# Row norms from 32-row blocks on four column tiles, a re-balanced order and a fourth buffer, in a residual quantizer kernel

## The chip, the cores and the metric

The kernel runs on one core of a Trainium2 chip. The metric is the device time of one execution in microseconds (us). The runs of the kernel before all lie between 754.28 and 757.95 us. All times compared here are of runs taken beside runs of the kernel before on the same chip. Engines: PE is TensorE (matmuls; PEld its weight loads), DVE is VectorE, ACT is ScalarE, POOL is GpSimd, SP issues the input transfers. PSUM is the memory that TensorE writes and VectorE and ScalarE read; the kernel uses it in banks of 512 columns, and emptying it is called an eviction. The trace gives the clock granted to TensorE as full or half (its records hold 1.0 or 0.5); "half clock" is the time spent at half.

## The reference

```python
# x: 2 x 16000 x 512 bf16; codebooks: 4 stages x 8 codes x 512
z = silu(depthwise_conv3(x, dw_enc))
res, q = z, 0
for s in range(4):
    d2 = norm2(res)[..., None] - 2 * res @ cb[s].T + norm2(cb[s])
    sel = cb[s][d2.argmin(-1)]
    q, res = q + sel, res - sel
return depthwise_conv3(q, dw_dec)
```

The norm of a row does not alter which code is nearest, but it takes part in the bf16 rounding of the distances, so the kernel computes it.

## The kernel before

The 32,000 rows go through in tiles of up to 16 groups of 128 rows. For each tile VectorE and ScalarE compute z (transposed: the 512 columns lie on partitions, four chunks of 128). Scores for stages 0 to 2 and the norms come from one "score block" on TensorE; stage 3, which needs the rounded residual, gets a second one. Between them lie 24 residual updates per tile: TensorE multiplies one-hot rows by codebooks into PSUM, and either VectorE adds the result to z (one matmul per PSUM bank) or ScalarE copies it back, for which TensorE must first add z itself with an identity matmul.

A score block for 8 row groups uses z as weights and as moving data, in blocks of 64 rows on two column tiles. The diagonal of each 64 x 64 product is the norm; a mask of -2^100 off the diagonal, laid down by one matmul per bank first, lets a maximum pick it out.

```python
# z buffer: [128, KT, 2*GM, 96]; each 64-row block carries its 32 codebook columns (times -2)
for u in range(nb):                  # row groups of this PSUM bank
    for i in range(KT):              # 4 chunks of 128
        for h in range(2):           # two column tiles of 64
            blk = Z[:, i, 2 * (g0 + nb * q + u) + h, :]
            nc.tensor.matmul(o[64 * h:64 * h + 64, u * w:(u + 1) * w],
                             lhsT=blk[:, NC:ZW], rhs=blk[:, c0:ZW], ...)   # 96 or 72 moving columns
# VectorE then empties it:
nc.vector.tensor_reduce(out=rr[0], in_=v[:, :, :, NC:ZW], axis=X, op=max)      # 64 wide
nc.vector.tensor_tensor(out=S, in0=v[:, :, :, 0:24], in1=CC2, op=add)
```

A list scheduler in the kernel file (class `Plan`) orders all steps with estimated costs. It has tuned ranks (`WHEN`), limits on evictions outstanding per engine (`QUOTA`), and a bias (`SHARE`) that decides whether a residual update is evicted by VectorE or ScalarE. Its estimates decide the order alone: in the program each engine's instructions then stand in that fixed order.

## Time and profile before

| | before |
|---|---|
| time, median of 3 | 756.12 us |
| VectorE busy / idle of the span | 719.4 / 35.0 us |
| ScalarE busy | 640.0 us |
| TensorE busy | 549.0 us |
| a score block, mask to last matmul, mean of 63 calls | 2.15 us |
| TensorE at half clock | 89 us |

The groups of instructions by shape of the kernel before; columns are line, engine, operation, output and inputs, shapes and count, then busy us and mean ns of one, then idle time of the engine before them and what ended it:

```profile
L626 ACT CAST ZB<-ps 128x1024 bf16<-128x1024 f32 x213 | 202.9, 1032 | 18.7 <-PE ps L620 17.2 <-ACT ZB L626 0.7 <-DVE rr L521 0.7
...
L628 DVE TENSOR_TENSOR ZB<-ZB,ps 128x1024 bf16<-128x1024 bf16 x123 | 146.8, 1210 | 5.0 <-PE ps L620 5.0
...
L521 DVE TENSOR_REDUCE rr<-ps 128x8 f32<-128x512 f32 x30 | 20.5, 682 | 1.7 <-PE ps L486 1.7
...
L645 DVE TENSOR_REDUCE rr<-ps 128x8 bf16<-128x512 f32 x30 | 20.4, 681 | 1.8 <-PE ps L486 1.8
```

An eviction costs VectorE 1210 ns and ScalarE 1032 (L628, L626). The two norm reductions take 682 ns each, and VectorE waited less than 2 us in all before each group of thirty: TensorE had the blocks ready. How far ahead it was shows in the timeline (start us, duration us, then as above; a bracket gives idle time and its cause). First VectorE, then TensorE (the second bank of a block and what follows it), of the same stretch of the kernel before:

```profile
390.67 0.74 DVE L446 TENSOR_SCALAR TA<-XT,WENC 128x2048 bf16<-128x2048 bf16 x1
391.33 1.41 DVE L446 TENSOR_SCALAR TB<-XT,WENC 128x2048 bf16<-128x2048 bf16 x2
392.65 0.68 DVE L521 TENSOR_REDUCE rr<-ps 128x8 f32<-128x512 f32 x1
```

### The profile page before, as it was taken

What the parts mean: (1) busy time and instruction counts of PE and PEld (TensorE: products, weight loads), DVE (VectorE), ACT (ScalarE), POOL (GpSimd) and SP (SyncE); (2) the same over time, 40 slices, a digit from 0 to 9 for tenths busy, and PEclk for the clock granted to TensorE, in tenths of its full rate; (3) what the DMA queues carried; (4) which work ended last, traced back from release to release, by engine and by line L of the source; (5) the groups of instructions that cost most, each with busy time, mean ns of one, the idle gap of its engine ahead of it and who ended that gap; (6) DMA issues with size and microseconds to landing.
All of it is one profiled execution on the core that took longest, in us unless ns stands there. A gap on an engine that the chain in (4) does not pass through costs nothing. (4 is left out here: it accounts for less than half of the span.)

```text
span 754.4 us, 15788 instructions
## 1 busy us (share of the span) xinstructions
PE 549.0 (73%) x6425; PEld 281.0 (37%) x6425; DVE 719.4 (95%) x1286; ACT 640.0 (85%) x549; POOL 131.8 (17%) x199
## 2 busy tenths in 40 slices
PE   1163667777786777888777778887777878898994
PEld 0131234243342434444343434444343434453442
DVE  8989999999999999999999999999999999989992
ACT  7776897939799698998989899898989899988575
POOL 2002212000120213112021212202131211111113
PEclk9996697999999999899999999999999999999998
DMA  5443434402333334242433424242432220212214
GB/s 114 98 99 76 117 60 111 99 9 57 84 113 84 114 77 148 50 106 86 97 120 73 146 57 121 70 112 93 91 128 56 101 54 30 85 56 86 85 56 149
DMA packets 148016, 67.27 MB, mean 89 GB/s; under 512 B 139776, under 2 KB 139808, under 8 KB 147944
## 3 DMA queue, kind: packets, MB, share of 16 engines
q1 hardware_dynamic: 137088, 33.06, 20.5%
q0 software_dynamic: 10640, 32.78, 12.7%
q8 instruction: 50, 0.82, 0.5%
q10 hardware_dynamic: 216, 0.43, 0.2%
q14 instruction: 22, 0.18, 0.1%
HBM read 0.43 MB, written 32.77 MB: 44 GB/s over the span
## 5 line engine op out<-in xcount | busy, mean ns | idle before, releaser
L620 PE MATMUL ps<-OHW,CBN 128*128 128x512 bf16 (+1 forms) x768 | 268.6, 391 | 42.4 <-DVE ZB L628 34.4
L626 ACT CAST ZB<-ps 128x1024 bf16<-128x1024 f32 (+2 forms) x281 | 236.2, 918 | 35.0 <-PE ps L620 32.6
L619 PE MATMUL ps<-ZB,IDENT 128*128 128x512 bf16 (+1 forms) x494 | 194.1, 393 | 36.3 <-DVE ZB L628 16.8
L628 DVE TENSOR_TENSOR ZB<-ZB,ps 128x1024 bf16<-128x1024 bf16 (+2 forms) x151 | 162.7, 1098 | 5.1 <-PE ps L620 5.0
L620 PEld LDWEIGHTS <-CBN 128*128 128x128 bf16 x768 | 76.2, 100 | 186.4 <-issue 122.5
L709 POOL DMA_DIRECT2D out_dram<-YB x130 | 70.1, 543 | 376.9 <-ACT YB L686 374.0
L686 ACT CAST YB<-ps 128x1024 bf16<-128x1024 f32 x126 | 121.4, 1031 | 17.0 <-PE ps L678 14.6
L455 ACT ACTIVATE EX<-ZB 128x4096 bf16<-128x4096 bf16 (+2 forms) x36 | 115.5, 3209 | 12.8 <-DVE ZB L298 11.7
L486 PE MATMUL ps<-ZB 128*64 128x96 bf16 (+1 forms) x4032 | 106.7, 210 | 21.3 <-DVE ZB L298 21.1
L486 PEld LDWEIGHTS <-ZB 128*64 128x64 bf16 x4032 | 90.0, 116 | 71.1 <-issue 42.1
L467 ACT ACTIVATE EX<-EX 128x4096 bf16<-128x4096 bf16 (+2 forms) x36 | 115.0, 3198 | 0.2
L678 PE MATMUL ps<-WDEC,OHW 128*128 128x512 bf16 x252 | 75.7, 391 | 28.4 <-DVE PR L543 6.9
L446 DVE TENSOR_SCALAR TB<-XT,WENC 128x2048 bf16<-128x2048 bf16 (+2 forms) x144 | 95.1, 678 | 0.0
L619 PEld LDWEIGHTS <-IDENT 128*128 128x128 bf16 x494 | 49.9, 101 | 64.7 <-issue 14.1
L298 DVE TENSOR_TENSOR ZB<-ZB,EX 128x4096 bf16<-128x4096 bf16 (+2 forms) x36 | 72.6, 2016 | 1.1 <-ACT EX L467 1.0
L298 DVE TENSOR_TENSOR TA<-TA,TB 128x4096 bf16<-128x4096 bf16 (+2 forms) x36 | 72.9, 2024 | 0.1
L298 DVE TENSOR_TENSOR ZB<-TA,TB 128x4096 bf16<-128x4096 bf16 (+2 forms) x36 | 72.5, 2014 | 0.0
L429 POOL COPY XT<-XT 128x508 bf16<-128x508 bf16 x18 | 36.3, 2018 | 124.3 <-DVE TB L446 120.8
L481 PE MATMUL ps<-MSK,IDENT 128*128 128x288 bf16 (+2 forms) x126 | 40.6, 323 | 20.4 <-DVE S L522 15.4
L455 ACT ACT_TABLE_LOAD x17 | 21.8, 1283 | 37.1 <-DVE ZB L298 37.0
L446 DVE TENSOR_SCALAR TA<-XT,WENC 128x2048 bf16<-128x2048 bf16 (+2 forms) x72 | 51.8, 728 | 0.4 <-issue 0.2
L678 PEld LDWEIGHTS <-OHW 128*128 128x128 bf16 x252 | 24.1, 99 | 60.8 <-issue 40.2
(92 smaller groups left out, 447.7 us busy)
## 6 DMA issues: line engine op xcount, KB each, us to landing
out_dram<-YB POOLq DMA_DIRECT2D x33, 448.0 KB, 3.4
out_dram<-YB POOLq DMA_DIRECT2D x28, 512.0 KB, 3.0
XT<-in_x_dram SPq DMA_TRANSPOSE x252, 2.8
out_dram<-YB POOLq DMA_DIRECT2D x30, 60.0 KB, 3.4
out_dram<-YB POOLq DMA_DIRECT2D x31, 2.0 KB, 2.8
out_dram<-YB POOLq DMA_DIRECT2D x2, 224.0 KB, 2.7
YB<-in_dw_dec_dram ACTq DMA_DIRECT2D x1, 384.0 KB, 3.9
out_dram<-YB POOLq DMA_DIRECT2D x1, 384.0 KB, 3.9
```

The source lines that it names most:

```text
L298: add("DVE", cost, key, lambda: nc.vector.tensor_tensor(out=out, in0=a, in1=b, op=op), reads, writes, **kw)
L446: return lambda: nc.vector.tensor_scalar(out=dst, in0=X[:, i, k:k + G, :].rearrange("p g c -> p (g c)"), scalar1=WENC[:, k, i:i + 1], scal ...
L455: add("ACT", act(2 * R), ("exp", n, h), lambda: nc.scalar.activation(v(ex), Z, ACT.Exp, scale=-1.0), zt, [("EX", sl), "ACTTAB"], hold="E")
L467: nc.scalar.add_instruction(mybir.InstActivation(name=nc.get_next_instruction_name(), engine=mybir.EngineType.Activation, func=ACT.Reciprocal,
L486: nc.tensor.matmul(o[HB * h:HB * h + HB, u * w:(u + 1) * w], lhsT=blk[:, NC:ZW], rhs=blk[:, c0:ZW], start=False, stop=(u == nb - 1 and i = ...
L619: nc.tensor.matmul(o.rearrange("p (k h c) -> p k h c", h=2, c=HB), lhsT=IDENT, rhs=zg[:, k0:k0 + nk], start=True, stop=False)
L620: nc.tensor.matmul(o, lhsT=CBN[s, u][:, i * P:(i + 1) * P], rhs=W[:, k0:k0 + nk, PADC:PADC + P], start=not on_act, stop=True)
L626: nc.scalar.copy(zg, v)
L628: nc.vector.tensor_tensor(out=zg, in0=zg, in1=v, op=ALU.add)
L678: nc.tensor.matmul(o, lhsT=W[:, k, PADC:PADC + P], rhs=WDEC[u], start=True, stop=not wrap)
L686: add("ACT", act(1024), key, lambda k=k, box=box, Y=Y, k0=k0: nc.scalar.copy(Y[:, 2 * (k - k0):2 * (k - k0) + 2, :].rearrange("p g d -> p ...
L709: nc.gpsimd.dma_start(out=view[p0:p1, lo:hi, :], in_=Y[p0:p1, lo - g0:hi - g0, :])
```

## The change

The intent was to cut VectorE's work in two ways. Row norms come from 32-row blocks, so that VectorE reduces over 32 columns instead of 64; TensorE uses four column tiles, with twice as many instructions of 64 moving columns each. And the order was re-tuned, moving 20 full evictions from VectorE to ScalarE. The codebook columns no longer stand in every z block but once per buffer, and a moving access pattern of two pieces joins them to the block. This makes z smaller and contiguous, one PSUM bank holds 8 row groups, and a fourth z buffer fits.

```diff
-    HB = P // 2
+    HB = 32
-    NX, NE, NZ, NOH, NY = 2, 3, 3, 4, 4
+    NX, NE, NZ, NOH, NY = 2, 3, 4, 4, 4
-    QUOTA = {"ACT": 2, "DVE": 2}
+    QUOTA = {"ACT": 2, "DVE": 1}
     (SHARE, SLACK and all ranks WHEN: other numbers; cut)
-    ZB = [sb([P, KT, 2 * GM, ZW], BF16, f"ZB{b}") for b in range(NZ)]
+    ZF = [sb([P, ZN + KT * NC], BF16, f"ZB{b}") for b in range(NZ)]
...
-                    for h in range(2):
-                        blk = Z[:, i, 2 * (g0 + nb * q + u) + h, :]
-                        nc.tensor.matmul(o[HB * h:HB * h + HB, u * w:(u + 1) * w], lhsT=blk[:, NC:ZW], rhs=blk[:, c0:ZW], ...)
+                    for q in range(P // HB):
+                        blk = Z[:, i, b0 + u, HB * q:HB * (q + 1)]
+                        at = (i * GM + b0 + u) * P + HB * q
+                        both = bass.AP(tensor=blk.tensor, offset=blk.offset, ap=[blk.ap[0], (ZN + i * NC - at, 2), (1, HB)])
+                        nc.tensor.matmul(o[HB * q:HB * (q + 1), u * ZW:(u + 1) * ZW]..., lhsT=blk, rhs=both, ...)
...
-                nc.vector.tensor_reduce(out=grp(rr[0], ...), in_=v[:, :, :, NC:ZW], axis=AX.X, op=ALU.max)
+                nc.vector.tensor_reduce(out=rr[0][:, g0:g1, 0], in_=v[:, :, 0:HB], axis=AX.X, op=ALU.max)
```

## The prediction

> **What bounds it now.** VectorE. The page's busy table has DVE at 719.4 us of the 754.4 us span (95%), ACT 640.0, PE 549.0. In windows of 42 us from 84 to 671 us DVE is 40.5 to 41.95 busy; tiles of 16 row groups follow each other every 43.3 us (spacing of the score matmuls in the timeline). DVE's 35 us of idle time lie mostly in the first two and the last windows (4, 3 and 17 us).
>
> **What changes, by durations from the trace.**
> 1. Row norms. The 60 full norm reductions read 8x64 PSUM columns in 682 ns; the 192-column score addition takes 346, the 64-column cast 213. Between these a column costs about 1.05 ns, so 8x32 should take about 415 ns: with the small tiles 16.4 us less DVE.
> 2. Residual evictions. The instruction order shows 20 full ones (and one small) moved from DVE (about 1.18 us busy each) to ACT (about 1.0): DVE -24 us, ACT +21. A middle tile has 7 instead of 8 on DVE.
> 3. Setup. Twelve ACT copies of codebook columns (1.08 us each) become 16 tiny ones: ACT -9 us, at the start.
> 4. PE. A score block goes from two column tiles of 96 or 72 moving columns to four of 64. A pair now repeats every 43 ns (96) or 33 ns (72), its halves 3 ns apart[...]. Four tiles should repeat every 30 to 38 ns: for 8 row groups 1.0 to 1.2 us plus a 0.22 us mask matmul, against 2.1 (96) and 1.75 (72) now: twice the instructions, yet about 35 us less PE over 60 calls; 40 more identity matmuls cost 9. PE isn't the limit. One PSUM bank instead of two per call and a fourth z buffer loosen waits.
> 5. Contiguous z changes no DVE rate: additions into strided z take 2280 ns, into contiguous TA 2282.
>
> **Sum.** DVE 719 - 16 - 24 = 679; ACT 640 + 21 - 9 = 652. A middle tile: DVE about 42.6 - 1.07 - 1.18 = 40.4, ACT about 38.8 + 1.0 = 39.8. Nearly level, so each has less slack to wait: I put the tile at 41.0 us, 2.3 less over 12 tiles = 28 us. Of the other 12 us of removed DVE work, at head and tail, I count 7. 756 - 35 = 721 us. Nearly all of the DVE saving is on the critical path; the PE saving hardly.
>
> **Prediction: 721 us, 8 in 10 between 708 and 737; faster by over 2%: 0.92, within 2%: 0.07, slower: 0.01.**
>
> **What would show it.** Right: norm reductions at 400 to 430 ns; DVE busy 675 to 685, still the fullest engine at about 94%; ACT 645 to 658; score quads 28 to 38 ns apart; middle tiles 40.5 to 41.5 us apart; DVE idle 38 to 48 us. Wrong: reductions over 500 ns; quads at 50 ns or more, with PE waits before the reductions; DVE idle over 60 us.
>
> **What would make it wrong.** Four column tiles might not load weights in parallel, and PE grow by over 60 us, delaying the decisions. DVE with only one eviction outstanding might wait for PE more often. With DVE and ACT level, each may stall on the other, leaving 735 to 745. Or the fourth buffer removes more idle time at head and tail than I count, to 705.

The 30 to 38 ns are the author's estimate. The trace of the kernel before alone leads to about the same: 24 columns more (96 against 72) cost a pair 10 ns, so 64 columns on two tiles would take about 30 ns, and two further tiles, each 3 ns behind as the second half of a pair is, about 36.

## More of the kernel before

```profile
389.66 0.34 PE L481 MATMUL ps<-MSK,IDENT 128*128 128x384 bf16 x1
389.92 0.87 PE L486 MATMUL ps<-ZB 128*64 128x96 bf16 x32
390.80 0.38 PE L619 MATMUL ps<-ZB,IDENT 128*128 128x512 bf16 x1
```

The block ends at 390.79 and VectorE starts to reduce it at 392.65. Over all 64 blocks the median of this lead is 1.85 us.

A few lines of the page of the kernel before: the span, each engine's busy time with its share of the span and its instructions, and the queue that fetches instructions (packets, MB, share of the transfer engines).

```profile
span 754.4 us, 15788 instructions
...
PE 549.0 (73%) x6425; PEld 281.0 (37%) x6425; DVE 719.4 (95%) x1286; ACT 640.0 (85%) x549; POOL 131.8 (17%) x199
...
q8 instruction: 50, 0.82, 0.5%
```

VectorE is busy 95% of the time: it is the limit. The last line looks harmless, but it matters later: queue q8 moved 50 packets of 16,384 bytes, and TensorE ran 12,850 instructions (6,425 matmuls and as many weight loads), about 257 to a packet.

## The result and the profile after

The changed kernel took 765.51 us (762.97 to 767.38, 4 runs) beside 755.75 us for the kernel before: a ratio of 1.0127, 95% interval 1.0093 to 1.0161. It is slower by 1.3%. (Ratios are the mean time of one kernel's runs over the mean of the other's in the same rounds, so not quite the ratio of the medians.)

The same lines of the page, and of the groups by shape, of the changed kernel:

```profile
span 765.6 us, 23805 instructions
...
PE 539.3 (70%) x10436; PEld 269.8 (35%) x10436; DVE 684.1 (89%) x1265; ACT 648.0 (85%) x574; POOL 132.3 (17%) x199
...
q8 instruction: 81, 1.33, 0.7%
```

```profile
L492 PE MATMUL ps<-ZB 128*32 128x64 bf16 x8064 | 92.9, 205 | 44.2 <-DVE ZB L306 22.9 <-issue 21.1
...
L644 DVE TENSOR_REDUCE rr<-ps 128x8 bf16<-128x256 f32 x30 | 12.5, 418 | 18.7 <-PE ps L591 9.7 <-PE ps L492 7.3 <-PE ps L559 1.3
L521 DVE TENSOR_REDUCE rr<-ps 128x8 f32<-128x256 f32 x30 | 12.5, 416 | 12.3 <-PE ps L492 10.8 <-PE ps L591 1.4
```

The work fell almost as predicted: a norm reduction takes 416 to 418 ns, VectorE is busy 684.1 us, ScalarE 648.0. But VectorE's idle time rose from 35.0 to 81.5 us, more than the 35.3 us of work that it lost. 31 us of its waits are now before the norm reductions (3.5 before), for TensorE. And TensorE's score matmuls have 21.1 us of idle time under "issue", which means time in which the engine waited for nothing that the profile shows; before they had none.

Such a stretch in the timeline of the changed kernel, TensorE first, then VectorE:

```profile
349.93 0.38 PE L492 MATMUL ps<-ZB 128*32 128x64 bf16 x25
351.14 1.58 PE L492 MATMUL ps<-ZB 128*32 128x64 bf16 x103 [0.83 <-issue]
352.65 1.89 PE L677 MATMUL ps<-WDEC,OHW 128*128 128x512 bf16 x4
354.33 0.50 PE L485 MATMUL ps<-MSK,IDENT 128*128 128x512 bf16 x1
354.75 0.33 PE L492 MATMUL ps<-ZB 128*32 128x64 bf16 x20
355.96 1.20 PE L492 MATMUL ps<-ZB 128*32 128x64 bf16 x108 [0.88 <-issue]
356.98 0.64 PE L591 MATMUL ps<-IDENT,OHA 128*32 128x128 bf16 x20
359.69 0.27 PE L591 MATMUL ps<-IDENT,OHA 128*32 128x128 bf16 x4 [2.08 <-issue]
```

```profile
352.75 0.42 DVE L521 TENSOR_REDUCE rr<-ps 128x8 f32<-128x256 f32 x1 [1.85 <-PE ps L492]
...
360.00 0.42 DVE L644 TENSOR_REDUCE rr<-ps 128x8 bf16<-128x256 f32 x1 [4.36 <-PE ps L591]
```

TensorE stops in the middle of a score block, between two matmuls that depend on nothing new, and again 256 instructions later (a matmul and its weight load are two). VectorE stands still behind it. The last reduction waits even for the transposes L591 behind its block: in the trace the block's last matmul sends no semaphore update of its own, the next update is that of the last transpose, and a stop had fallen between them.

Counting TensorE's matmuls and weight loads in the trace shows where the stops fall. 21 gaps of more than 0.6 us without a wait (from the start of one instruction to that of the next) add up to 28.9 us. The longest is 2.33 us. All 21 end at the same place in the count, 191 past a multiple of 256, so they lie whole multiples of 256 instructions apart; queue q8 moved 81 packets (called refills below) for TensorE's 20,872 instructions, about 258 to a packet. The packet of q8 before each stop's end starts 2.26 to 2.9 us before TensorE goes on. Two packets never start less than 3.35 us apart, while an undisturbed score block of 8 row groups runs its 256 score instructions in 1.22 us. In the kernel before there is no such gap at all. That TensorE waits there for its next packet is inferred from these counts and times; no record names the cause.

**Theory.** The doubled score instructions outrun the instruction fetch, and the stops land on VectorE because the re-balanced order has taken away the lead that used to hide such things. **Rivals.** (a) The re-tuned order or the levelled engines alone: each stalls on the other. (b) 32-wide column tiles are slow. (c) The fourth buffer starts transfers earlier, which then collide with others (the share of busy transfer engines in the middle windows rose from about 0.37 to about 0.5). (d) TensorE's half-clock time, up from 89 to 116 us.

### The profile page after: what moved, and what is told of

The parts are those of the page before. It is cut to its first block, busy times and chain, and to the rows that moved or that the text cites. A ratio compares the mean times of both kernels' runs of the same rounds, so it can differ in the third digit from the quotient of the medians.

```text
span 765.6 us, 23805 instructions
## 1 busy us (share of the span) xinstructions
PE 539.3 (70%) x10436; PEld 269.8 (35%) x10436; DVE 684.1 (89%) x1265; ACT 648.0 (85%) x574; POOL 132.3 (17%) x199
## 4 chain that ended last, share of the span: by engine, by line
DVE 59%; PE 26%; issue 8%; ACT 4%; DMA 1%; SPq 1%; DVEq 0%; POOL 0%; POOLq 0%; ACTq 0%
DVE ZB L627 12%; DVE ZB L306 11%; DVE TB L455 8%; PE ps L492 8%; PE ps L619 7%; DVE TA L306 6%; PE ps L618 5%; DVE TA L455 4%; DVE EX L465 3%; PE ps L677 2%; DVE OHW L595 2%; PE ps L485 2%; DVE KEY L306 2%; DMA XT<-in_x_dram 1%; ACT YB L685 1%
## 5 line engine op out<-in xcount | busy, mean ns | idle before, releaser
L625 ACT CAST ZB<-ps 128x1024 bf16<-128x1024 f32 (+2 forms) x302 | 257.6, 938 | 56.2 <-PE ps L619 54.8
L618 PE MATMUL ps<-ZB,IDENT 128*128 128x512 bf16 (+1 forms) x535 | 210.0, 393 | 28.7 <-DVE ZB L627 10.3
L708 POOL DMA_DIRECT2D out_dram<-YB x130 | 79.4, 615 | 435.3 <-ACT YB L685 432.5
L627 DVE TENSOR_TENSOR ZB<-ZB,ps 128x1024 bf16<-128x1024 bf16 (+2 forms) x130 | 139.0, 1087 | 6.4 <-PE ps L619 5.9
L685 ACT CAST YB<-ps 128x1024 bf16<-128x1024 f32 x126 | 126.3, 1038 | 13.3 <-PE ps L677 12.5
L492 PE MATMUL ps<-ZB 128*32 128x64 bf16 x8064 | 92.9, 205 | 44.2 <-DVE ZB L306 22.9
L492 PEld LDWEIGHTS <-ZB 128*32 128x32 bf16 x8064 | 81.3, 100 | 106.2 <-issue 82.3
L485 PE MATMUL ps<-MSK,IDENT 128*128 128x512 bf16 (+1 forms) x64 | 26.8, 419 | 29.9 <-DVE S L522 14.5
L437 POOL COPY XT<-XT 128x508 bf16<-128x508 bf16 x18 | 19.4, 1081 | 143.8 <-DMA XT<-in_x_dram 122.6
L465 DVE TENSOR_SCALAR EX<-EX 128x4096 bf16<-128x4096 bf16 (+2 forms) x36 | 39.0, 1083 | 1.0 <-ACT EX L464 1.0
L438 POOL COPY XT<-XT 128x508 bf16<-128x508 bf16 x18 | 30.7, 1706 | 47.4 <-DVE TB L455 38.5
```

The lines of the kernel that those rows point to most:

```text
L492: nc.tensor.matmul(o[HB * q:HB * (q + 1), u * ZW:(u + 1) * ZW].rearrange("p (s c) -> p s c", s=2), lhsT=blk, rhs=both, start=False, stop=( ...
L618: nc.tensor.matmul(o, lhsT=IDENT, rhs=zg[:, k0:k0 + nk, :], start=True, stop=False)
L625: nc.scalar.copy(zg, v)
L627: nc.vector.tensor_tensor(out=zg, in0=zg, in1=v, op=ALU.add)
L685: add("ACT", act(1024), key, lambda k=k, box=box, Y=Y, k0=k0: nc.scalar.copy(Y[:, 2 * (k - k0):2 * (k - k0) + 2, :].rearrange("p g d -> p ...
L708: nc.gpsimd.dma_start(out=view[p0:p1, lo:hi, :], in_=Y[p0:p1, lo - g0:hi - g0, :])
```

## The experiments

### 1. Half the score instructions (e1_half)

Two column tiles of 64 weights, each with the two pieces of 32 moving columns. Half the norms are wrong. VectorE and ScalarE run the same instructions in the same order as in the changed kernel.

```diff
-                    for q in range(P // HB):
-                        blk = Z[:, i, b0 + u, HB * q:HB * (q + 1)]
-                        at = (i * GM + b0 + u) * P + HB * q
+                    for q in range(2):
+                        blk = Z[:, i, b0 + u, 64 * q:64 * (q + 1)]
+                        at = (i * GM + b0 + u) * P + 64 * q
```

> The changed kernel with its score blocks on two column tiles of 64 weights (moving pieces still 2 x 32 columns): half the score instructions of TensorE (4,032 weight loads and 4,032 matmuls instead of 8,064 each), same array time per block, same order and sizes on every other engine. The norms of half the rows are wrong on purpose; the sizes read from PSUM are not. Instruction fetch theory (TensorE runs out of instructions at 16 KB boundaries): refills fall from 81 to about 50, the no-wait gaps vanish, VectorE idle falls from 81 us to about 40, 718 to 732 us. Rival (the new order, or VectorE and ScalarE being level, makes each stall on the other): 758 to 770 us.

Measured: 738.19 us (ratio to before 0.9762, interval 0.9739 to 0.9785). From the page of this run, the busy times and the instruction queue:

```profile
PE 531.0 (72%) x6404; PEld 265.6 (36%) x6404; DVE 684.1 (93%) x1265; ACT 646.7 (88%) x574; POOL 132.0 (18%) x199
...
q8 instruction: 50, 0.82, 0.5%
```

The gaps fell from 21 to one, and VectorE's idle time from 81.5 to 52.3 us at the same busy time, 684.1. So the count of instructions costs 27 us of the changed kernel (765.5 to 738.2), and rival (a) alone is refuted. The clock is no part of this: half-clock time is 111 us here and 116 in the changed kernel. But it is not all: the figure lies between the two expectations, 17 us above the prediction.

### 2. Twice the score instructions in the kernel before (e2_before_quads)

```diff
-                    for h in range(2):
+                    for h in range(4):
                         blk = Z[:, i, 2 * (g0 + nb * q + u) + h // 2, :]
-                        ...matmul(o[64 * h:64 * h + 64, ...], lhsT=blk[:, NC:ZW], rhs=blk[:, c0:ZW], ...)
+                        r0 = NC + 32 * (h % 2)
+                        ...matmul(o[32 * h:32 * h + 32, ...], lhsT=blk[:, r0:r0 + 32], rhs=blk[:, c0:ZW], ...)
```

> The kernel before with each 64-row score matmul split into two of 32 rows on four column tiles, all with the same moving columns (96 or 72): twice the score instructions, about the same array time (a quad about 6 ns longer than a pair), the same result, schedule and work on every other engine. Instruction fetch theory: about 81 refills, stalls of 0.5 to 2.3 us at some of them, VectorE idle up by 15 to 45 us, 770 to 800 us. Rival (schedule or balance): 754 to 760 us, as before.

Measured: 760.55 us (ratio 1.0055, 1.0031 to 1.0078), correct. This misses the fetch theory's expectation and lies just above the rival's. The waits of this run (who waited for whom: us in total, times, longest):

```profile
PE ps L487 <- issue: 25.2, 24, 2.4
...
DVE rr L646 <- PE ps L487: 6.0, 5, 2.3
...
DVE rr L522 <- PE ps L487: 3.9, 3, 2.8
```

The stops are all there: 81 refills, 27 gaps, 34.0 us in sum, more than in the changed kernel. Yet they cost about 4 us. So the stops alone don't explain the loss; the kernel before absorbs them, and the changed kernel does not. That made the second half of the theory, the lead, the question to test. The run also speaks against rival (b): its quads of 96 columns repeat every 42 to 43 ns, just as the pairs of the kernel before do.

### 3 and 4. The old ranks, and three z buffers (e3_old_schedule, e4_three_z)

The changed kernel with `SHARE`, `SLACK`, `QUOTA` and `WHEN` of the kernel before; and the changed kernel with `NZ` = 3.

> The changed kernel with the ranks, shares, slacks and quotas of the kernel before. Schedule theory: the new numbers are the fault, the time falls to 720 to 735 us. Instruction fetch theory: the score bursts stay as dense, so the time stays at 750 to 785 us, with 81 refills and no-wait gaps of 20 to 40 us in sum.

> The changed kernel with three z buffers instead of four. If the fourth buffer is the fault (earlier loads, DMA share 0.5 instead of 0.37 in the middle windows): 745 to 758 us. Instruction fetch theory: the fourth buffer is not the fault, 762 to 785 us.

Measured: 803.46 us (1.0627) and 835.49 us (1.1041), both correct, both with 81 refills. Both are far worse than the changed kernel and outside all their expected ranges. They tell little: the scheduler makes a different order from each set of numbers, and these sets were not tuned for it, so the two runs clear neither the new numbers nor the fourth buffer. Half-clock time was 161 and 218 us. Against rival (c) speak other runs: experiment 1 keeps the fourth buffer and transfer engines as busy (0.39 to 0.55 in the windows from 213 to 553 us, 0.42 to 0.52 in the changed kernel) and gains 27 us, and experiment 12 will show the stops with three buffers. For the other 17 us rival (c) is not excluded.

### 5. Empty instructions put back (e5_pad)

Experiment 1 with a second matmul after each (the same 64 weights, one moving column of zeros).

> The half-instruction kernel (738 us) with, after each pair of score matmuls, a pair of matmuls with the same 64 weights and one moving column of zeros, added to a score that they don't change: as many TensorE instructions as the changed kernel (8,064 score matmuls), still 64-wide column tiles. Norms wrong on purpose as before. Fetch theory: the count of instructions is what costs, so refills return to about 81, the gaps of 0.5 to 2.3 us at 256-instruction boundaries come back, 755 to 775 us. Rival (32-wide column tiles are slow or drain the array): no gaps, 736 to 745 us.

Measured: 815.4 us (1.0782), wrong. It is outside both expected ranges. As a control for rival (b) it failed, because it was not clean: each pair now repeats every 63 ns instead of 32, so a score block is slower by itself, and the refill gaps are only 7 (9.5 us). Nothing is claimed from it on 32-wide tiles. Yet it shows something: blocks longer by 1.37 us on average (3.08 against 1.71) cost 77 us over 64 calls. In this order, a microsecond in a score block is nearly a microsecond of the kernel, though part of the loss may be the clock: half-clock time rose from 111 to 206 us.

### 6 and 7. Shorter score blocks in both orders (e8_quarter, e9_before_half)

Only two of the four chunks in each block: once in experiment 1's kernel, once in the kernel before. Their outputs are wrong, which doesn't matter for the times.

```diff
-                for i in range(KT):
+                for i in range(2):
```

> The half-instruction kernel (738 us) with only two of the four chunks of the row length in each score block: a quarter of the changed kernel's score instructions, half the array time of a block. Wrong on purpose; sizes and order on all other engines unchanged. Theory that VectorE has no lead over TensorE in the new order, so each us of a score call is on the path: a call falls by 0.5 to 0.6 us (0.5 x 60 = 30 us), so 708 to 728 us. Rival (VectorE and ScalarE are level and stall on each other, the score calls are not on the path): 733 to 740 us.

> The same cut made in the kernel before: two of four chunks, half the score instructions, a call shorter by about 0.9 us. Wrong on purpose. Theory that the kernel before has VectorE as its limit and its score blocks done well ahead: 750 to 757 us, although 60 x 0.9 = 54 us of TensorE time are gone. Rival (score calls are on the path there too): 700 to 735 us.

Measured: 729.98 us (0.966) and 754.52 us (0.9992, 0.9975 to 1.0008). The second is as expected: TensorE lost 0.65 us in each of 64 score blocks and the kernel before is not measurably faster. The first fell by 8 us, less than the expected 10 to 30, and lies between the ranges of theory and rival. The runs with score blocks of different length together, each from its own trace (lead: median time from the last score matmul to the reduction):

| kernel | score block, mean us | lead, us | VectorE busy / idle us | half clock, us | time us |
|---|---|---|---|---|---|
| e9, old order | 1.50 | 2.53 | 719.7 / 33.0 | 144 | 754.5 |
| before, old order | 2.15 | 1.85 | 719.4 / 35.0 | 89 | 755.8 |
| e2, old order | 2.62 | 1.56 | 719.5 / 38.1 | 90 | 760.6 |
| e8, new order | 1.16 | 1.39 | 683.8 / 45.6 | 148 | 730.0 |
| e1, new order | 1.71 | 1.04 | 684.1 / 52.3 | 111 | 738.2 |
| after, new order | 2.16 | 0.89 | 684.1 / 81.6 | 116 | 765.5 |
| e5, new order | 3.08 | 0.68 | 684.9 / 130.7 | 206 | 815.4 |

(The first score block of a run, which waits long for its data, is left out of the means.) In the old order, 1.1 us per block, 72 us in all, moves the time by 6 us. In the new order the first 0.55 us per block (35 us in all) cost 8 us, the next 0.45 us (29 us) cost 27 us, and the next 0.92 us (59 us) cost 50. This reads as if the lead were a reserve: while it lasts, TensorE's time is nearly free, and when it is used up, TensorE's time counts almost in full. It is a reading, for no run changed the lead alone, and e5 has the most half-clock time as well. Half-clock time does not order these runs: e8 has more of it than the changed kernel and is 35 us faster. That speaks against rival (d) as the cause here; it was not taken away by itself.

### 8 to 11. Orders that know of the refills (e6, e7, e10, e11)

The `Plan` class got a limit on how fast TensorE may pass 256 instructions (the refill limit) and a model of the clock, and the ranks were searched anew; e10 and e11 have a finer model of the clock than e6 and e7. The numbers in both were the author's estimates, and no trace showed them as such; they are left out here and cut from the expectations of e6 and e10. What the trace of the changed kernel shows: stops that follow each other after 256 instructions end 3.49 to 5.1 us apart. e6 and e11 issue a block in two pieces, between which other TensorE work may stand. All correct.

> The changed kernel with the same tile work, correct result, but each score block issued in two pieces of four row groups that other TensorE work may stand between, and with an order that was searched again with a planning model[...]. Fetch theory: the same 81 refills, but gaps at the boundaries under 15 us in sum, and VectorE idle under 60 us: 722 to 745 us. If the order cannot hide the refills: 750 to 770 us.

> As the kernel with pieces, but with whole score blocks of eight row groups: only the order is new, searched with the refill limit in the planning model. Fetch theory: some of the gaps stay, since a block of 258 instructions always crosses one boundary; sum of gaps 10 to 30 us, 730 to 752 us. If order does not matter and only the count does: 760 to 770 us.

> The changed kernel, correct result, whole score blocks of eight row groups; only the order is new. It was searched with a planning model that has the refill limit and also the clock as the traces show it[...]. If refills and half-clock windows together are what the order of the changed kernel missed: 730 to 750 us, half-clock time under 90 us. If the planning model still misses something: 755 to 775 us.

> The same search for score blocks in two pieces of four row groups, correct result. Same two theories: 728 to 748 us, or 752 to 770 us; against the earlier kernel with pieces (755 us, 153 us at half clock) the half-clock time should fall.

Measured: 755.43 us (0.9997, 0.9972 to 1.0022), 773.17 us (1.0223), 766.3 us (1.0156) and 761.87 us (1.0079). All four missed the hoped-for range. With pieces, e6 cut the sum of gaps to 15.0 us (11 gaps) and gained 10 us on the changed kernel, but half-clock time rose to 153 us and VectorE still idled 72 us. Whole blocks, e7, kept gaps of 37 us. The two with the finer model of the clock still had 162 and 144 us at half clock. So the planning model still misses something, and what, stays open.

### 12. The norms alone, in the old order (e12_norms_old_order)

The kernel before, three buffers, two banks, with only the 32-row norms. The scheduler is given the old costs, so that VectorE and ScalarE run the same instructions in the same places.

```diff
+    RB = 32
+    PW = NC + RB
-                    for h in range(2):
+                    for h in range(P // RB):
                         blk = Z[:, i, 2 * (g0 + nb * q + u) + h // 2, :]
-                        ...matmul(..., lhsT=blk[:, NC:ZW], rhs=blk[:, c0:ZW], ...)
+                        r0 = NC + RB * (h % 2)
+                        both = bass.AP(tensor=blk.tensor, offset=blk.offset, ap=[blk.ap[0], (r0, 2), (1, RB)])
+                        ...matmul(..., lhsT=blk[:, r0:r0 + RB], rhs=both, ...)
```

> The kernel before, its order, its three z buffers and its PSUM banks, with only the row norms changed: score blocks of 32 rows on four column tiles, two-piece moving read, norm reductions over 32 columns. Correct result. Order on VectorE and ScalarE is that of the kernel before, instruction for instruction. Theory that VectorE still has a lead in this order, so the doubled score instructions cost about 4 us as in the run with quads: VectorE busy falls by 16 us to about 703 and most of it shows, 741 to 750 us, faster than both kernels. Rival (the lead goes with the saved work, and the refill stalls then land on VectorE): 753 to 765 us.

Measured: 748.3 us (ratio 0.9886, 0.987 to 0.9903), correct. It beats both kernels: 1.1% under the kernel before, and by the medians 2.2% under the changed one. Its busy times, from the page, and then its groups by shape:

```profile
PE 532.5 (71%) x10423; PEld 270.5 (36%) x10457; DVE 703.4 (94%) x1286; ACT 638.8 (86%) x549; POOL 131.0 (18%) x199
```

```profile
L491 PE MATMUL ps<-ZB 128*32 128x64 bf16 x8064 | 98.2, 201 | 52.2 <-issue 30.7 <-DVE ZB L300 21.2 <-ACT ZB L631 0.2
...
L650 DVE TENSOR_REDUCE rr<-ps 128x8 bf16<-128x256 f32 x30 | 12.6, 419 | 4.8 <-PE ps L491 4.8
L526 DVE TENSOR_REDUCE rr<-ps 128x8 f32<-128x256 f32 x30 | 12.6, 419 | 2.2 <-PE ps L491 2.1
```

TensorE stops more than in the changed kernel (30.7 us of "issue" before the score matmuls against 21.1), yet VectorE waited 7 us before the reductions instead of 31: its lead is 1.68 us. VectorE's work fell by 16.0 us, and half of that arrived.

### 13 and 14. The evictions moved, without the new order (e13_norms_true_costs, e15_moved_late)

e13 is experiment 12 with the true costs given to the scheduler, which then moves 18 evictions to ScalarE. e15 is experiment 12 with every seventh VectorE eviction given to ScalarE after the order is fixed, so that nothing else moves:

```diff
+        order = plan.order()
+        mine = [s["take"][1] for s in order if s["take"] and s["dest"] == "ANY" and s["take"][1]["dest"] == "DVE"]
+        for box in mine[6::7]:
+            box["dest"] = "ACT"
```

> The same kernel, but the planning model is told the shorter norm reductions, so it moves 18 evictions from VectorE to ScalarE as the change did, with the old ranks. Theory that levelling the two engines is what uses up the lead: VectorE busy about 682, idle over 70 us, 755 to 790 us, slower than the same norms in the old order. Rival (levelling is harmless): 725 to 742 us.

> The kernel with the 32-row norms in the old order (748 us), with every seventh of the 151 evictions on VectorE (21) given to ScalarE after the order is fixed: nothing else changes place on any engine. Correct result. This is the second half of the predicted VectorE saving without a new order. If levelling itself is harmless: VectorE busy about 679, ScalarE about 660, 722 to 738 us. If levelling takes away VectorE's lead, so that TensorE's refill gaps land on it: 742 to 765 us.

Measured: 811.59 us (1.0728) and 767.42 us (1.0139, 1.011 to 1.0167), both correct, each above even its slower expected range. e13 is inconclusive: as in experiment 3, old ranks with other costs gave a poor order altogether. e15 is the clean one. VectorE's largest waits, first those of experiment 12, then those of e15, and last e15's busy times from its page:

```profile
DVE rr L650 <- PE ps L491: 7.1, 6, 2.3
...
DVE ZB L633 <- PE ps L625: 4.9, 8, 1.4
```

```profile
DVE ZB L633 <- PE ps L625: 23.5, 30, 4.1
...
DVE ZB L300 <- ACT EX L470: 9.5, 11, 1.8
```

```profile
PE 548.2 (72%) x10495; PEld 274.7 (36%) x10495; DVE 686.9 (90%) x1265; ACT 655.2 (86%) x570; POOL 131.6 (17%) x199
```

VectorE has 16.5 us less to do than in experiment 12, and the kernel is 19 us slower. VectorE's idle time rose from 43.3 to 77.9 us, close to the 81.5 of the changed kernel. It now waits for TensorE before its evictions (23.5 us against 4.9), and for ScalarE (9.5 us). So levelling the two engines is enough to expose VectorE, without a new order.

But it does not happen as the theory says. The lead before the norm reductions is still 1.49 us (1.68 in experiment 12, 0.89 in the changed kernel). And in the traces, of VectorE's waits over 0.15 us, those that overlap a stop or the microsecond after it are 30.2 of 65.3 us in the changed kernel, 11.0 of 27.8 in experiment 12 and 16.7 of 62.0 in e15. So most of what e15 adds is not the stops: it looks like rival (a), each engine stalling on the other. No run takes this apart, for instance e15 with half the score instructions. One more caution: ScalarE's extra evictions stand in places chosen for VectorE, and a better place may exist; experiment 1 shows that with half the instructions the levelled engines can reach 738 us.

## Why the prediction was wrong

It said 721 us (708 to 737) and faster; measured was 765.5, slower by 1.3%.

- **Right, the work:** reductions at 416 to 418 ns (predicted 400 to 430), VectorE busy 684.1 (675 to 685), ScalarE 648.0 (645 to 658). Contiguous z indeed changed no rate: additions into it take 2280 to 2295 ns, about 2282 before.
- **Right, the array:** undisturbed, four column tiles repeat every 32 ns (28 to 38 predicted). In a long run the two further tiles cost hardly anything: two tiles of 64 columns repeat every 31 to 32 ns too (experiment 1). What the two-piece moving read costs is not separated.
- **Wrong, the step "twice the instructions, yet about 35 us less PE over 60 calls".** A score block averages 2.16 us against 2.15 before. The prediction costed array time and not the supply of instructions. The trace before shows about 257 instructions to a packet and no two packets under 3.78 us apart; there that could be mere demand, since TensorE never stopped for one. The changed kernel, which does stop, has them no closer than 3.35 us, and a block of 258 instructions in about 1.2 us asks for nearly three times that. Taking the instructions away gives 27 of the missing 44 us (experiment 1).
- **Wrong, the step "Nearly all of the DVE saving is on the critical path; the PE saving hardly".** The second part was true of the kernel before (experiment 7) and false of the changed one, where 28.9 us of stops cost 27 us. It took the slack of the old profile into a kernel whose purpose was to use that slack up. The same doubling cost 4 us in the old order (experiment 2). Why the new order does not hide the stops, its shorter lead, is argued from the table and was not tested alone. Levelling by itself also cost the VectorE saving its effect (experiment 14, e15), mostly in waits that no stop touches.
- **Mis-sized, the level engines' stalling and the ends.** The sum leaves VectorE 42 us of idle time in all. Without the stops (experiment 1) VectorE idles 52.3 us and is busy 684.1, 5 more than the sum had: a span of 736.4 us, 738 of time. The place of the loss can be read from the traces. From the first norm reduction of the third tile to that of the fourteenth, 11 tiles take 472.8 us before (43.0 each), 473.9 in the changed kernel (43.1) and 453.0 in experiment 1: 41.2 each, inside the predicted 40.5 to 41.5. Two misses cancel there: VectorE idles 1.3 us a tile and not 0.6, but works 39.9 us and not 40.4. The rest of the span, head and tail, takes 281.6 us before, 291.7 in the changed kernel and 283.4 in experiment 1, where the prediction counted 7 us less: against the kernel before, VectorE's work there fell by 6 us and not 12, and its idle time rose from 29.9 to 37.8. The prediction named the stalling as a risk ("735 to 745") but gave it too little weight. The risk of slow weight loads did not occur (TensorE was busy 539.3 us, 549.0 before), nor that of one outstanding eviction: VectorE waited 5.8 us before its full evictions, 5.0 before.

What remains open: why orders planned with the refill limit do not reach 738 us, and how much of that is half-clock time; what in the new order lets the stops through; and where the waits of e15 come from.

## What to carry to other kernels

When a change multiplies small instructions, divide the instructions of its densest burst by the rate at which a trace shows instruction blocks to arrive, as you would for data; here a burst of 256 took 1.22 us and packets were never less than 3.35 us apart, and that, not the array time, was the limit. Take the rate from a trace in which the engine stops for them: one without stops shows only its own demand. Before you give work from a full engine to a half-empty one, ask how far ahead the engines that feed it run: in a fixed order a lead can hide their stops (in experiment 2, 34.0 us of stops cost about 4 us), and here it was about halved (1.85 to 0.89 us) when the order was re-tuned. If one part of a change needs no new order, try it alone in the old one: here the norms alone beat the whole.
